# An FFT mixer with two MLPs: conversion slots, stores and first rows at the end of the columns

## The chip, the cores and the metric

The kernel runs on one core of one Trainium2 chip. The metric is the device time of one execution in microseconds (us). Its engines are TensorE (PE, matrix products, with weight loads shown as PEld), VectorE (DVE), ScalarE (ACT), GpSimd (POOL) and SyncE (SP), which here only issues transfers. Each engine and each issuing queue works through its instructions in order.

## The reference

Three blocks follow one another on an input of 4 batches, 3136 positions and 256 channels, all float32.

```python
X = np.fft.rfft(x, axis=1)
x = np.fft.irfft(X * (filt_r + 1j * filt_i)[None], n=3136, axis=1)
h = x.transpose(0, 2, 1) @ U @ V                 # rank 32, along the sequence
u = x + h.transpose(0, 2, 1)
x = u + np.maximum(u @ w_ch1, 0) @ w_ch2         # 256 -> 1024 -> 256
mu, var = x.mean(-1, keepdims=True), x.var(-1, keepdims=True)
xn = (x - mu) / np.sqrt(var + 1e-6) * g_ln
return x + np.maximum(xn @ w2_ch1, 0) @ w2_ch2   # the second MLP has its own weights
```

## The kernel before

The FFT over 3136 positions is done in factors, as matrix products with tables. Batch 0 goes through class `First` ahead of everything else: `rows` makes the first factor, seven steps; `columns` the other factors, the filter and the way back. The result of batch 0 lies in DRAM, `bd[0]`; from there it is read in units of 448 positions (tile `wt`, with a table `ic`). `unit` makes the last factor of the way back, adds `h`, and splits the sum into a high and a low float32r part (`ah`, `al`). The two layers of the MLP (`m1` L792, `m2` L811 to L820) use three products for each, high by high, high by low and low by high. The other three batches run their FFT between the steps of the MLPs.

The weights V, w1, w2 and those of the second MLP come as 64-bit words and are converted on the chip, 18 jobs, in the generator `stagger`: each `next(pr)` is a slot. The first four slots only ask for the words of the first jobs. After them every fourth slot (PACE) starts a job, and every slot moves all jobs under way by one step (`to32`): two copies on ScalarE (L947, L948), four word operations on VectorE (L934 to L940, one slot each), a product and a sum on GpSimd (L952, L954), two idle slots, the high part on ScalarE (L224), the low part (L1026 for weights, L1070 for V). The low part is made on VectorE up to the end of the columns, on GpSimd after that. Jobs 0 and 1 are V; their parts are stored in `vd` (L1061), the low one a slot after it is made, and `load_v` (L1079) reads both back into `v_sb`, issued by GpSimd. `fetch` asks for the words of coming jobs (L928); during the columns it does not go past six. How many slots pass at which place is set by hand: FETCHES and FETCH, ROWSLOTS (a slot for each entry, after that step of the rows), COLSLOTS (so many after each step of the columns).

`columns` works on seven pairs, the last pair first, in ten steps. Step j runs `across` of pair 6-j (transposes L677 into two PSUM banks, copied by ScalarE to `z0`), `forward` of pair 7-j (L689 into two of three rotating PSUM banks; then `filtered`: four products on VectorE, L631 and L636, and four combinations on GpSimd, L638 and L639), and `back` of pair 9-j (L650, then `pt` L657; both need the combinations). For odd indices the products go to rotating tiles `hl` and `hh`, three each, which V's low and high parts use as well. After `back` ScalarE copies the two banks to `be`, a part of `big`, and four stores (L668) go to `bd[0]`, by SP; for pair 0 VectorE makes one of the copies and ScalarE issues two of the stores. Steps 0 to 3 also hold the stages of U (`u_half`: transpose, products, `uf` on VectorE, four copies `uq` on ScalarE). Each step also asks for the filters of a later pair (L602, for the last pair L610 too).

At pair 0, ahead of its own stores, `load_unit` (L729) asks for units 0 and 1: their tables, and the rows from QUICK on, which come from the other six pairs. After the columns follow `finish(0)` (the sum of `pt`, split into `tk`), `late_rows` (L735, the first QUICK rows of units 0 and 1, which pair 0's stores write), the words up to job 7, REST constant products on TensorE (L1172), and then units 0 and 1 and the main loop, with two slots in each step.

## Time and profile before

| what | value |
|---|---|
| median of 3 runs | 1335.75 us (1335.61 to 1335.92) |
| the profiled execution | 1335.85 us |
| its span, first to last instruction | 1334.0 us |
| mean granted TensorE clock | 0.996 of 2.4 GHz |
| TensorE busy | 98% of the span |
| VectorE, ScalarE, GpSimd busy | 60%, 32%, 11% |

All times of the rows are counted from the first instruction. A row of a time line has start, duration, engine, line, operation, what is written from what, and how many instructions were merged into it; in square brackets stands how long the engine sat idle before it and what ended that.

### The profile page before, as it was taken

Reading aid. Unit: us, or ns where it says so; the run is one execution under the profiler, and the core shown is the slowest. Engines: PE = TensorE matmul, PEld = TensorE weight load, DVE = VectorE, ACT = ScalarE, POOL = GpSimd, SP = SyncE. Lnnn points to the kernel's source line nnn. Section 1 sums busy time; section 2 is a strip of 40 time slices with the busy share of each in tenths; the row PEclk is TensorE's granted clock in tenths of the full one; section 3 lists DMA queues with packets and bytes.
Section 4 is the critical chain, followed back from the end, with each engine's and each line's share of the span. In section 5 each row is a group of like instructions: output and inputs, shape, how many; then the busy total and the mean of one; then the engine's idle time right before and its main releaser. Section 6 shows DMA issues by size and latency. Waiting matters only on the chain.

```text
span 1334.0 us, 23246 instructions
## 1 busy us (share of the span) xinstructions
PE 1308.9 (98%) x9018; PEld 1039.6 (78%) x9018; DVE 798.0 (60%) x1620; ACT 424.3 (32%) x831; POOL 149.3 (11%) x128
## 2 busy tenths in 40 slices
PE   8899999999999999999999999999999999999998
PEld 8477677776877877777777877878888888888887
DVE  6937885666656556566565565565455545555454
ACT  4535642333322323323232232232222222222222
POOL 1716540112000011010000010100000000000000
PEclk9899999999999999999999999999999999999999
DMA  9753446576554254453555454522102212210121
GB/s 253 201 160 118 125 126 196 167 209 190 137 179 149 72 145 141 124 145 90 153 171 142 133 168 105 152 78 65 39 27 65 65 18 65 65 44 5 48 48 40
DMA packets 166999, 154.24 MB, mean 116 GB/s; under 512 B 65801, under 2 KB 142473, under 8 KB 166889
## 3 DMA queue, kind: packets, MB, share of 16 engines
q1 hardware_dynamic: 166348, 151.12, 40.8%
q0 software_dynamic: 288, 1.40, 0.5%
q8 instruction: 71, 1.16, 0.4%
q14 instruction: 40, 0.32, 0.1%
q10 hardware_dynamic: 252, 0.23, 0.1%
HBM read 92.71 MB, written 48.97 MB: 106 GB/s over the span
## 4 chain that ended last, share of the span: by engine, by line
PE 87%; DVE 6%; DMA 2%; ACT 2%; issue 1%; POOL 1%; SPq 1%; DVEq 0%; POOLq 0%; ACTq 0%
PE psh L792 38%; PE pso L819 13%; PE pso L820 7%; PE pso L811 6%; PE pso L812 6%; PE pso L813 6%; PE psu L769 2%; PE ps L316 2%; PE ps L390 1%; PE ps L356 1%; PE psu L774 1%; DVE hl L796 1%; PE pt L396 1%; PE ps L650 1%; PE pz L531 1%
## 5 line engine op out<-in xcount | busy, mean ns | idle before, releaser
L796 DVE SCALAR_TENSOR_TENSOR hl<-psh,hh 128x512 fp32r<-128x512 f32 (+1 forms) x400 | 271.7, 680 | 366.2 <-ACT hh L795 365.3
L795 ACT ACTIVATE hh<-psh 128x512 fp32r<-128x512 f32 (+1 forms) x400 | 235.3, 589 | 666.6 <-PE psh L792 666.5
L819 PE MATMUL pso<-wb,hh 128*128 128x512 f32 x784 | 285.0, 397 | 0.7 <-DVE x L834 0.3
L792 PE MATMUL psh<-ah,wb 128*128 128x512 f32 (+1 forms) x800 | 280.1, 391 | 1.9 <-DVE hl L796 1.9
L820 PE MATMUL pso<-wb,hl 128*128 128x256 f32 x784 | 219.8, 280 | 0.0
L792 PEld LDWEIGHTS psh<-ah,wb 128*128 128x128 f32 x800 | 149.8, 188 | 47.6 <-issue 5.3
L819 PEld LDWEIGHTS pso<-wb,hh 128*128 128x128 f32 x784 | 147.3, 188 | 36.2 <-DVE x L834 1.6
L792 PE MATMUL psh<-ah,w1h 128*128 128x512 f32 (+1 forms) x400 | 157.7, 394 | 2.1 <-ACT ah L224 2.1
L811 PE MATMUL pso<-hh,w2h 128*128 128x512 f32 (+1 forms) x400 | 156.7, 392 | 1.0 <-ACT hh L795 0.7
L812 PE MATMUL pso<-hl,w2h 128*128 128x512 f32 (+1 forms) x400 | 154.3, 386 | 2.0 <-DVE hl L796 2.0
L792 PE MATMUL psh<-al,w1h 128*128 128x512 f32 (+1 forms) x400 | 156.0, 390 | 0.2
L792 PE MATMUL psh<-al,wb 128*128 128x512 f32 (+1 forms) x400 | 155.6, 389 | 0.0
L813 PE MATMUL pso<-hh,w2l 128*128 128x512 f32 (+1 forms) x400 | 154.3, 386 | 1.1 <-POOL w2l L1026 1.1
L792 PE MATMUL psh<-ah,w1l 128*128 128x512 f32 (+1 forms) x400 | 154.9, 387 | 0.0
L820 PEld LDWEIGHTS pso<-wb,hl 128*128 128x128 f32 x784 | 148.0, 189 | 7.7 <-DVE hl L796 0.3
L372 POOL TENSOR_TENSOR xs<-xs,ft 128x512 f32<-128x512 f32 x42 | 56.9, 1355 | 643.6 <-DMA xs<-zc 356.4
L792 PEld LDWEIGHTS psh<-ah,w1h 128*128 128x128 f32 x400 | 75.5, 189 | 24.6 <-issue 4.0
L859 DVE SCALAR_TENSOR_TENSOR x2t<-pso,ln,x2t 128x256 f32<-128x256 f32 x196 | 89.7, 479 | 3.7 <-PE pso L820 0.2
L811 PEld LDWEIGHTS pso<-hh,w2h 128*128 128x128 f32 x400 | 75.1, 188 | 21.5 <-issue 5.9
L812 PEld LDWEIGHTS pso<-hl,w2h 128*128 128x128 f32 x400 | 75.2, 188 | 17.6 <-DVE hl L796 2.7
L813 PEld LDWEIGHTS pso<-hh,w2l 128*128 128x128 f32 x400 | 75.2, 188 | 16.7 <-POOL w2l L1026 1.7
L792 PEld LDWEIGHTS psh<-ah,w1l 128*128 128x128 f32 x400 | 75.6, 189 | 15.9
(144 smaller groups left out, 1318.9 us busy)
## 6 DMA issues: line engine op xcount, KB each, us to landing
ft<-flt SPq DMA_DIRECT2D x42, 512.0 KB
xd<-x SPq DMA_DIRECT2D x96, 128.0 KB
x2t<-xd SPq DMA_DIRECT2D x24, 512.0 KB
wt<-bd SPq DMA_DIRECT2D x52, 224.0 KB
out<-x2t SPq DMA_DIRECT2D x84, 128.0 KB
xs<-zc SPq DMA_DIRECT2D x168, 64.0 KB
xt<-x SPq DMA_DIRECT2D x84, 112.0 KB
zd<-ze SPq DMA_DIRECT2D x84, 112.0 KB
```

Of the source, the lines that this page charges most:

```text
L316: nc.tensor.matmul(pss[j][quarter(h), m * D:(m + 1) * D], ct[rows56(j), 2 * h + m], xs[h][rows56(j), m], start=True, stop=True)
L372: nc.gpsimd.tensor_tensor(out=xs, in0=xs, in1=fi[:, e], op=ALU.mult)
L769: nc.tensor.matmul(pss[h][c * HALF:(c + 1) * HALF, dh, h * spare + m:h * spare + half:UW], t[rows, m, d0:d0 + HALF], ic[rows, m, :], start ...
L792: nc.tensor.matmul(ps[:, :n], w[:, kt, fs], a[:, kt, :n], start=j == 0, stop=j == 3 * KT - 1)
L795: nc.scalar.activation(out=hh[:, :n], in_=ps[:, :n], func=AF.Relu)
L796: nc.vector.scalar_tensor_tensor(out=hl[:, :n], in0=ps[:, :n], scalar=0.0, in1=f32(hh[:, :n]), op0=ALU.max, op1=ALU.subtract)
L811: nc.tensor.matmul(o, wh[:, f, ds], hh[:, :n], start=f == 0, stop=False)
L812: nc.tensor.matmul(o, wh[:, f, ds], hl[:, :n], start=False, stop=False)
L813: nc.tensor.matmul(o, wl[:, f, ds], hh[:, :n], start=False, stop=f == FT - 1)
L819: nc.tensor.matmul(o, hh[:, cs], w, start=f == 0, stop=False, skip_group_check=True)
L820: nc.tensor.matmul(o[:, D:], hl[:, cs], w[:, :D], start=False, stop=f == FT - 1, skip_group_check=True)
L859: nc.vector.scalar_tensor_tensor(out=o, in0=acc[c][:, half * D:(half + 1) * D], scalar=rs[:, c:c + 1], in1=o, op0=ALU.mult, op1=ALU.add)
```

## The change

In the rows, three of nine slots are taken out. In the columns the slots are 2 in steps 0 to 5 and 1 in steps 6 to 9 (16), where they were 2, 3, 3, 3, 3, 1 (15). Six slots (WAIT) are run behind the columns, after `finish(0)` and the first rows, and ahead of the constant products, of which 24 are left of 48. So 28 slots have passed when the main loop begins, where it was 24. The limit of six on words fetched in the columns is gone, and with it the fetch up to job 7 after them. A pair's four groups of rows leave in two stores, one for each half, out of one piece of `big` that holds both groups; the bytes are the same. The tables of units 0 and 1 are asked for at pair 1, behind its stores; their rows from QUICK on at pair 0, behind its stores; the first rows where they were.

```diff
-ROWSLOTS = (1, 2, 2, 3, 4, 5, 5, 5, 6)
-COLSLOTS = (2, 3, 3, 3, 3, 1)
+ROWSLOTS = (1, 2, 2, 3, 4, 5)
+COLSLOTS = (2, 2, 2, 2, 2, 2, 1, 1, 1, 1)
-REST = 48
+REST, WAIT = 24, 6
@@ back(p)
-                to = bd[0].rearrange("(j a s g p) w -> a g j p s w", j=2, a=n // 2, s=2, g=2)[p]
+                to = bd[0].rearrange("(j a g p) w -> a j p g w", j=2, a=n // 2, g=4)[p]
+                be = self.big[:, p % 2, 4 * D * ((p + 1) // 2):4 * D * ((p + 3) // 2)]
+                for g in range(2):
+                    (nc.vector.tensor_copy if p == 0 and g else acopy)(
+                        be.rearrange("p (s g k q) -> p s g k q", s=2, g=2, k=KT)[:, :, g], pss[g].rearrange("p (s q k) -> p s k q", s=2, k=KT))
+                for h in range(2):
+                    (nc.scalar if p == 0 and h else nc.sync).dma_start(to[h], be[rows56(h)].rearrange("p (g w) -> p g w", g=4))
+                if p == 1:
+                    for u in range(2):
+                        wt[u] = new_unit(u)
                 if p == 0:
-                    load_unit(0)
-                    load_unit(1)
-                for g in range(2):
-                    at = BLK * (p + 1)
-                    be = self.big[:, g, at:at + BLK]
-                    (nc.vector.tensor_copy if p == 0 and g else acopy)(be.rearrange("p (s k q) -> p s k q", s=2, k=KT),
-                                                                       pss[g].rearrange("p (s q k) -> p s k q", s=2, k=KT))
-                    for h in range(2):
-                        (nc.scalar if p == 0 and h else nc.sync).dma_start(to[g, h], be[rows56(h)].rearrange("p (s w) -> p s w", s=2))
+                    for u in range(2):
+                        first_rows(u, QUICK, QT)
@@
-    def late_rows():
+    def first_rows(u, a, z):
         rows = bd[0].rearrange("(h q m) w -> h q m w", h=2, m=NM)
+        for h in range(2):
+            nc.sync.dma_start(wt[u][0][h * HALF + a:h * HALF + z], rows[h, a:z, UW * u:UW * u + UW])
@@ stagger
-                fetch(min(i + 2, 6) if held.get("columns") else i + 2 if i > 1 else i + 1)
+                fetch(i + 2 if i > 1 else i + 1)
@@ after the columns
-        late_rows()
-        held.pop("fetch")(8)
+        for u in range(2):
+            first_rows(u, 0, QUICK)
+        for _ in range(WAIT):
+            next(pr)
         warm = inner("warm")
         for _ in range(REST):
             nc.tensor.matmul(warm[:, :P], ones, ones, start=True, stop=True)
```

## Rows read from the trace of the kernel before

**Rows 1.** The page: busy time, share of the span and instructions of each engine.
```profile
PE 1308.9 (98%) x9018; PEld 1039.6 (78%) x9018; DVE 798.0 (60%) x1620; ACT 424.3 (32%) x831; POOL 149.3 (11%) x128
```

**Rows 2.** Time line of TensorE, from the constant products on.
```profile
76.64 10.98 PE L1172 MATMUL warm<-ones 128*128 128x128 f32 x96
87.56 1.15 PE L769 MATMUL psu<-ic,wt 56*64 56x56 f32 x64
88.64 0.74 PE L774 MATMUL psu<-v_sb,tk 96*128 96x256 f32 x4
...
90.44 1.14 PE L769 MATMUL psu<-ic,wt 56*64 56x56 f32 x60 [0.80 <-DVE al L227]
...
93.22 0.50 PE L792 MATMUL psh<-ah,w1h 128*128 128x512 f32 x1 [0.98 <-ACT ah L224]
...
101.01 0.50 PE L813 MATMUL pso<-hh,w2l 128*128 128x512 f32 x1 [1.07 <-POOL w2l L1026]
```

**Rows 3.** Time line of the SP queue, at the end of the columns.
```profile
73.68 1.67 SPq L668 DMA_DIRECT2D bd<-big  x4
...
77.06 0.80 SPq L729 DMA_DIRECT2D wt<-bd  x2
...
80.49 1.83 SPq L668 DMA_DIRECT2D bd<-big  x2
84.61 1.29 SPq L735 DMA_DIRECT2D wt<-bd  x4
```

**Rows 4.** Stretches: busy time (instructions) of each engine, clock, DMA share, GB/s.
```profile
30.00:40.00 10.00, 6.11 (x87) 4.02 (x88) 8.47 (x11) 6.10 (x13) 6.19 (x7) 0.95 0.98 263
```

**Rows 5.** Time line of TensorE, in the columns.
```profile
30.42 1.14 PE L677 MATMUL psz<-ident,big 128*120 128x128 f32 x8 [1.26 <-ACT z L224]
...
39.52 1.96 PE L677 MATMUL psz<-ident,big 128*120 128x128 f32 x8 [3.20 <-ACT z L224]
...
67.34 1.07 PE L689 MATMUL ps<-z,s_sb 56*32 56x256 f32 x24 [0.95 <-DVE hh L636]
```

**Rows 6.** Time line of ScalarE, in the columns.
```profile
29.19 0.68 ACT L948 ACTIVATE cyl<-stg 128x512 f32<-128x512 uint32 x1
...
50.68 1.59 ACT L224 ACTIVATE uq<-uf 64x224 f32<-64x224 f32 x4 [2.71 <-DVE uf L572]
```

**Rows 7.** Time line of VectorE, in the columns and behind them.
```profile
47.45 0.69 DVE L631 TENSOR_TENSOR hl<-ps,f 128x512 f32<-128x512 f32 x1 [1.36 <-PE pt L657]
...
60.88 0.68 DVE L631 TENSOR_TENSOR hl<-ps,f 128x512 f32<-128x512 f32 x1
...
80.56 0.42 DVE L227 TENSOR_TENSOR tk<-tt,tk 32x256 fp32r<-32x256 f32 x1 [0.50 <-ACT tk L224]
...
97.60 0.42 DVE L940 TENSOR_SCALAR cyh<-ct 128x512 int32<-128x512 int32 x1
...
101.27 1.67 DVE L938 SCALAR_TENSOR_TENSOR ct<-cyh,ct 128x512 int32<-128x512 int32 x1
```

**Rows 8.** Time line of GpSimd, in the columns.
```profile
58.09 1.18 POOL L639 TENSOR_TENSOR ya<-ya,xs 128x256 f32<-128x256 f32 x1
...
62.03 1.30 POOL L1079 DMA_DIRECT2D v_sb<-vd  x2
...
65.39 1.18 POOL L639 TENSOR_TENSOR ya<-ya,xs 128x256 f32<-128x256 f32 x1
67.34 0.73 POOL L638 TENSOR_TENSOR hl<-hl,hh 128x256 f32<-128x256 f32 x1 [0.76 <-DVE hh L636]
...
70.09 0.74 POOL L638 TENSOR_TENSOR hl<-hl,hh 128x256 f32<-128x256 f32 x1
```

**Rows 9.** The last filter loads (SP time line); the landing of V's load (tile `vd`).
```profile
57.91 1.81 SPq L610 DMA_DIRECT2D f<-flt  x4
...
DMA to landing us min/median/max: 7.0/7.3/7.6
```

**Rows 10.** Stretches: TensorE busy (instructions), granted clock, DMA share, GB/s.
```profile
40.00:42.00 2.00, 2.00 (x15) 0.50 1.01 295
```

More of the change, by code (lines that the diff above doesn't have):

```diff
@@ L727, in load_unit @@
         for h in range(2):
-            q = QUICK if i < 2 else 0
-            nc.sync.dma_start(wt[i][0][h * HALF + q:h * HALF + QT], rows[h, q:, m0:m0 + UW])
-    def late_rows():
+            nc.sync.dma_start(wt[i][0][rows56(h)], rows[h, :, m0:m0 + UW])
+    def first_rows(u, a, z):
         rows = bd[0].rearrange("(h q m) w -> h q m w", h=2, m=NM)
-        for i in range(2):
-            for h in range(2):
-                nc.sync.dma_start(wt[i][0][h * HALF:h * HALF + QUICK], rows[h, :QUICK, UW * i:UW * i + UW])
+        for h in range(2):
+            nc.sync.dma_start(wt[u][0][h * HALF + a:h * HALF + z], rows[h, a:z, UW * u:UW * u + UW])
     def unit(i):
@@ L975, in fetch @@
                 fetched += 1
-        held["fetch"] = fetch
         for n in range(4):
```

## The prediction

> **What bounds the kernel now.** I read the page's busy table first: TensorE works 98% of the span [rows 1], so what is left lies where TensorE waits, and the diff touches only the first hundred microseconds. The time line of TensorE there [rows 2] shows the largest piece: after the last pair of columns it runs 48 constant products from 76.64 to 87.6, and unit 0 begins at 87.56 without a wait of its own. The SP queue tells what the products cover [rows 3]. The last pair leaves TensorE just before 76.64. Its first half's store stands behind two loads of tables and four of rows; those rows wait for the store of the pair before (issued up to 75.35, landed by 77.06, so 1.7 us), and the last store goes out only from 80.49 to 82.32. The rows that need it are asked for at 84.61, 2.3 us later. Then the time line inside the columns: TensorE waits 1.26 us at 30.42 and 3.20 us at 39.52 for ScalarE's copies, and 0.95 us at 67.34 for VectorE [rows 5], which has each pair's products behind two or three conversion slots. After unit 1, which waits 0.80 us for unit 0's split, the first layer begins at 93.22 and waits once for a converted weight, 1.07 us at 101.01 [rows 2].
>
> I sum in times of this profiled execution: 1335.85 us, of which 1334.0 are the span; it lies 0.10 us over the median of the runs shown. A shift of the first layer's start moves the end by as much, since TensorE has no slack behind it.
>
> **Slots in the rows and columns.** A job takes a new slot in four; its ScalarE copies are in its slot 0, VectorE's four word operations in 1 to 4, GpSimd's product and sum in 4 and 5, the high and low parts in 8 and 9. Six slots instead of nine pass before the columns. I count nothing for the rows themselves, where TensorE fills its waits with constant products. But slot 8 (a high part of V and two word copies) no longer stands ahead of the first column copy on ScalarE, which it holds up until 29.87 [rows 6], and the wait at 30.42 [rows 5] shrinks by about 1.15 us. In step 1 the same three copies come back between U's copies and the next column copy, so the 3.20 us wait stays, only 1.15 us sooner.
> Step 3 takes that away again. Slot 12 now falls there: V's second high part and two word copies queue on ScalarE behind U's four copies (50.68, 1.59 us [rows 6]), and VectorE's low part waits for them. Adding these up, I get pair 3's products at 54.4, about where they were. From step 4 on there are two slots where there were three, then one. Pair 2's products come at 59.1 instead of 60.88 [rows 7]. They could be at 58.7, but the three rotating tiles `hl` now hold V's parts at other places, and the first product must wait for TensorE's `pt` of two pairs earlier, as at 47.45, where that costs 1.36 us [rows 7]. Pair 1's follow near 64 and pair 0's near 67. If nothing else held them, the columns would end 2.3 us sooner, near 74.4.
>
> **A wait that is new: `load_v` on GpSimd.** It is still issued after step 4. Before, V's low part had long been stored by then, and the two issues took 1.30 us without a wait [rows 8]. Now that part is made in slot 13 and stored in slot 14, in the same step, and on SP it stands behind a pair's stores and the last eight filter loads, 3.6 us of issues of which the second half is 57.91 to 59.72 [rows 9]. By my times it goes out at 59.9. V's own load took 7.0 to 7.6 us to landing, for far more bytes [rows 9]; the bd stores above 1.7 to 2.3. I take 2.3, the nearest in size, hence 62.2. GpSimd is through with pair 3 at 59.1 (before: 58.09 + 1.18) and waits 3.1 us. Behind the wait stand pair 2's four combinations, a conversion's product and sum, and pair 1's four, and TensorE's back products wait for the combinations. Their prices [rows 8]: 1.30 for the issues, 3.2 for pair 2 (63.33 to 66.57), 2.8 for product and sum (59.27 to 62.03, which used to lie ahead of the load), 2.8 for pair 1 (67.34 to 70.09), in all 72.3; it was 70.09. The back products of pair 1 then start at 70.9 and have their second half's input at 72.3. So the columns end near 76.8: **0.1 us later**, with 74.4 the end without the wait.
>
> **The stores and the first rows.** Merging four stores into two keeps the bytes; both copies must be done before either store, which costs part of a copy, and two issues are saved. On SP the order is now: pair 1's two stores, two tables (0.42 an issue, as the stores of [rows 3]), a load of 512 KB of words that the lifted limit of six lets through (it waits for slot 20's copies on ScalarE, until about 76.4), the last pair's store at 77.0 to 77.4 instead of 80.49, and the four loads of rows that began at 77.06, now to 79.1. The store lands between 79.1 (1.7 us) and, behind the words, 80.0; I take 80.0. First rows: two issues for unit 0 in 0.7 us (four took 1.29 [rows 3]), and landing 1.7 us later at the earliest, 82.4. The other bound is the queue: tables, words, stores and rows are some 2.06 MB from 75.6 on. At the 263 GB/s that a full stretch moved [rows 4] that is 7.8 us, 83.4, and 83.9 with the rest of a landing; at three quarters of that rate 86. I take 83.7, near the full stretch. The 24 products left take 5.5 us (half of 10.98 [rows 2]), end at 82.3 and no longer cover it: TensorE idles 1.4 us. Unit 0 starts at **83.7 instead of 87.56: 3.9 us won.**
>
> **Six slots ahead of unit 0.** They give VectorE six word operations, ScalarE three copies and GpSimd three operations, all behind `finish`, whose last VectorE operation ended at 80.98 [rows 7]. A word operation takes 0.42 alone and up to 1.67 beside GpSimd [rows 7]: 2.5 to 10 us for six, of which at most the last three have GpSimd beside them; I take 4.8, so VectorE is free at 86.0. It wants unit 0's split about when unit 0's products (1.15 + 0.74 [rows 2]) and ScalarE's copy are done, 85.9. Unit 1 needs that split, so **0.3 us lost** (0 to 2.5). The four slots more bring job 4's low weight to completion here, and the wait at 101.01 goes: **1.07 us won.** Later conversions run two steps ahead of where they were; their words are loaded in time either way, and I price that at nothing. Uncovered it would be another wait like that one.
>
> **Sum:** 1335.85 - 3.9 + 0.3 - 1.07 = **1331.2 us**. The columns' 0.1 lies in the 83.7. With the bounds of the landing (82.4 to 86) and of VectorE the likeliest case runs from 1329.6 to 1333.9.
>
> **Rivals.**
> No wait at `load_v` (the store lands while GpSimd is still busy): the columns and SP's order move 2.3 us ahead, **1328.9**. For it: SP could reach the store sooner than I add up. Against: it is behind eight filter loads in a strict order. 22%.
> The clock falls in the gap: with 24 products fewer TensorE has nothing for 1.4 us, and units 0 and 1 are small products with waits. After 3.20 us of idling the granted clock was 0.50, 1.2 GHz [rows 10], and a group of 1.14 us took 1.96 [rows 5]. If it falls by 83, the two units' 1.15 + 0.74 us each [rows 2] grow by 0.72 of themselves, 2.7 us: **1333.9**. Against: the 1.26 us of idling at 30.42 cost nothing that shows. 20%. The Trainium skill (TensorE: Matmul & The Clock Gate, Part 1: The HAM clock gate) states that the throttled state is the default and that activity releases it. By that rule the removed products are a risk and not only a saving, and the result is this rival's; the trace agrees that the clock falls after idling [rows 10].
> `load_v` waits longer: each microsecond past 59.4 goes to the columns' end through GpSimd. Once the store lands after 63.4, TensorE idles over 3 us ahead of pair 1's back products, as at 39.52, and the last 5.9 us of the columns run at 1.2 GHz, 0.72 of that or about 4 us more. At 63.4 this gives 1331.2 + 1.2 + 4 = 1336.4, and at a landing like the longest of V's, 7.6 us [rows 9], 1340.5; between them, **slower: 1338.4**. For it: the queue is full there. Against: 196 KB is a small store. 10%.
>
> **How the numbers follow.** The likeliest case has 48%. The measurement can tell about 0.2% (2.7 us) from no change: faster is below 1333.1. That takes nearly all of the likeliest case and of the first rival and a little of the second, 0.72; slower is the last rival, 0.10; the rest is 0.18. The range 1328.0 to 1334.9 leaves out the slower rival and the edges of the others.
>
> **What would show it.** After: one wait of GpSimd for a `vd` store of about 3 us ahead of `v_sb`, the columns' last `pt` near 76.8, the last store issued near 77, first rows issued near 80, unit 0 at 83 to 84 after a short idle time, the first layer near 89.5, no wait for `w2l`. It is wrong if the columns end near 74.4 (no wait on GpSimd), if the units' products run at 1.2 GHz, if unit 0 starts past 86, or if the units' splits wait for VectorE by more than 1 us.

## The result and the profile after

The changed kernel takes 1344.34 us (median of 4 runs, 1342.6 to 1348.88), the kernel before 1335.68 beside it: 1.007 of the time, 95% interval 1.0045 to 1.0096. By the medians it is **slower by 0.65%**, where 1331.2 was forecast.

The profiled execution after is the longest of the four, 1348.88 us, 4.5 above their median, and its stretches have that in them. I cut the profiled executions at four places on TensorE's time line: the first transpose of the columns (28.09 before, 31.46 after), the first constant product, unit 0, and the first product of the first layer.

| stretch, us | before | forecast | after |
|---|---|---|---|
| columns | 48.55 | 48.7 | 51.69 |
| columns' end to unit 0 (gap) | 10.92 | 6.9 | 9.03 |
| units 0 and 1 | 5.66 | 6.0 | 8.30 |
| first layer to the end | 1240.8 | 1239.7 | 1246.6 |
| span | 1334.0 | 1329.4 | 1347.1 |

The 3.4 us by which the columns begin later are this execution's: two runs that differ only behind the columns (e2 and e9 below) begin them at 28.59 and 28.86, all but one of the others at 27.6 to 30.5. The page, busy times, the line that answers to [rows 1]:

```profile
PE 1313.4 (97%) x8970; PEld 1039.6 (77%) x8970; DVE 797.5 (59%) x1620; ACT 424.8 (32%) x831; POOL 148.8 (11%) x128
```

Time line of TensorE after, answering to [rows 2, 5]:

```profile
32.77 1.14 PE L679 MATMUL psz<-ident,big 128*120 128x128 f32 x8 [0.25 <-ACT z L224]
41.88 1.96 PE L679 MATMUL psz<-ident,big 128*120 128x128 f32 x8 [3.20 <-ACT z L224]
...
75.76 0.66 PE L650 MATMUL ps<-hl,d 64*64 64x256 f32 x8 [2.47 <-POOL hl L638]
...
83.15 5.62 PE L1173 MATMUL warm<-ones 128*128 128x128 f32 x48
92.18 2.39 PE L769 MATMUL psu<-ic,wt 56*64 56x56 f32 x64 [3.40 <-DMA wt<-bd]
94.50 1.22 PE L774 MATMUL psu<-v_sb,tk 96*128 96x256 f32 x4
96.58 1.96 PE L769 MATMUL psu<-ic,wt 56*64 56x56 f32 x60 [0.47 <-DVE al L227]
98.47 1.22 PE L774 MATMUL psu<-v_sb,tk 96*128 96x256 f32 x4
100.47 0.79 PE L792 MATMUL psh<-ah,w1h 128*128 128x512 f32 x1 [0.78 <-ACT ah L224]
```

The two waits at the top of the columns are as forecast. New are 2.47 us ahead of pair 1's way back, 3.40 ahead of unit 0, and durations: a unit's products take 1.96 to 2.39 and 1.22 where they took 1.15 and 0.74. GpSimd's and SP's time lines, answering to [rows 3, 8, 9]:

```profile
67.72 1.30 POOL L1078 DMA_DIRECT2D v_sb<-vd  x2 [6.33 <-issue]
```
```profile
60.81 1.81 SPq L610 DMA_DIRECT2D f<-flt  x4
63.15 0.38 SPq L1060 DMA_DIRECT2D vd<-vl  x1
...
82.77 0.40 SPq L928 DMA_DIRECT2D stg<-w  x1
83.46 0.34 SPq L664 DMA_DIRECT2D bd<-big  x1
83.89 6.71 SPq L735 DMA_DIRECT2D wt<-bd  x8
```

GpSimd is free at 67.72 - 6.33 = 61.39 and waits for V's low part, stored at 63.15; it can go on 4.6 us after that issue. The last store goes out 0.3 us after the columns' end, as forecast, but the eight loads of rows behind it last until 90.6, since the last four wait for it. Stretches after, answering to [rows 4, 10]: the clock stands at 0.50, 1.2 GHz, in pair 1's way back and again from unit 0 into the first layer. A row here has the stretch, its length, the busy time and number of instructions of TensorE, its weight loads, VectorE, ScalarE and GpSimd, then the clock.

```profile
78.00:80.00 2.00, 2.00 (x20) 0.50 (x16) 0.00 (x0) 0.84 (x2) 2.00 (x3) 0.50 0.23 82
...
82.00:92.00 10.00, 6.78 (x70) 5.79 (x60) 7.57 (x13) 4.42 (x9) 2.75 (x3) 0.97 0.85 244
...
100.00:105.00 5.00, 4.53 (x10) 3.43 (x11) 2.00 (x5) 2.29 (x6) 0.00 (x0) 0.50 0.00 0
```

In the kernel before, too, the clock stands at 0.50 for a while, in the first layer behind units whose waits were 0.80 and 0.98 us:

```profile
94.00:97.00 3.00, 3.00 (x8) 2.32 (x9) 0.56 (x2) 0.93 (x3) 0.00 (x0) 0.50 0.00 0
```

The next unit's split is waited for longer than before, first before and then after, and behind that wait the clock of the changed kernel falls once more:

```profile
107.79 0.50 PE L792 MATMUL psh<-ah,w1h 128*128 128x512 f32 x1 [1.10 <-ACT ah L224]
```
```profile
114.97 0.54 PE L792 MATMUL psh<-ah,w1h 128*128 128x512 f32 x1 [2.09 <-ACT ah L224]
```
```profile
115.50:118.50 3.00, 2.98 (x8) 2.39 (x8) 1.09 (x2) 0.81 (x2) 0.00 (x0) 0.50 0.35 104
```

Last, TensorE's waits in the main loop between 160 and 192 us: three in the kernel before,

```profile
163.22 0.50 PE L812 MATMUL pso<-hl,w2h 128*128 128x512 f32 x1 [1.77 <-DVE hl L796]
178.52 1.09 PE L316 MATMUL ps<-xt,ct 56*64 56x256 f32 x14 [0.56 <-DVE hl L796]
179.93 0.50 PE L792 MATMUL psh<-ah,wb 128*128 128x512 f32 x1 [0.33 <-DVE hl L796]
```

and five in the changed kernel, 5.3 us in place of 2.7:

```profile
164.92 0.50 PE L812 MATMUL pso<-hl,w2h 128*128 128x512 f32 x1 [0.26 <-DVE hl L796]
169.34 1.98 PE L1034 MATMUL psw<-wg,ones 128*128 128x512 f32 x4 [1.62 <-DVE hl L796]
173.67 0.50 PE L792 MATMUL psh<-ah,w1h 128*128 128x512 f32 x1 [0.96 <-DVE hl L796]
184.81 0.50 PE L812 MATMUL pso<-hl,w2h 128*128 128x512 f32 x1 [1.10 <-DVE hl L796]
191.37 0.50 PE L792 MATMUL psh<-ah,wb 128*128 128x512 f32 x1 [1.38 <-DVE hl L796]
```

### The profile page after: what moved, and what is told of

It reads as the page before. It is cut to its first block, busy times and chain, and to the rows that moved or that the text cites. A ratio compares the mean times of both kernels' runs of the same rounds, so it can differ in the third digit from the quotient of the medians.

```text
span 1347.1 us, 23130 instructions
## 1 busy us (share of the span) xinstructions
PE 1313.4 (97%) x8970; PEld 1039.6 (77%) x8970; DVE 797.5 (59%) x1620; ACT 424.8 (32%) x831; POOL 148.8 (11%) x128
## 4 chain that ended last, share of the span: by engine, by line
PE 87%; DVE 4%; DMA 3%; ACT 2%; POOL 2%; issue 1%; SPq 1%; DVEq 0%; POOLq 0%; ACTq 0%
PE psh L792 37%; PE pso L819 13%; PE pso L820 6%; PE pso L811 6%; PE pso L812 6%; PE pso L813 6%; PE psu L769 2%; PE ps L316 2%; PE ps L390 1%; PE psu L774 1%; PE ps L356 1%; PE ps L650 1%; PE pz L531 1%; PE pt L396 1%; DVE hl L796 1%
## 5 line engine op out<-in xcount | busy, mean ns | idle before, releaser
L796 DVE SCALAR_TENSOR_TENSOR hl<-psh,hh 128x512 fp32r<-128x512 f32 (+1 forms) x400 | 271.6, 680 | 369.4 <-ACT hh L795 368.3
L792 PE MATMUL psh<-ah,wb 128*128 128x512 f32 (+1 forms) x800 | 280.0, 391 | 2.0 <-DVE hl L796 2.0
L792 PEld LDWEIGHTS psh<-ah,wb 128*128 128x128 f32 x800 | 149.7, 188 | 47.6 <-issue 5.3
L792 PE MATMUL psh<-ah,w1h 128*128 128x512 f32 (+1 forms) x400 | 158.5, 396 | 3.8 <-ACT ah L224 2.9
L792 PE MATMUL psh<-al,w1h 128*128 128x512 f32 (+1 forms) x400 | 156.5, 391 | 0.0
L792 PE MATMUL psh<-al,wb 128*128 128x512 f32 (+1 forms) x400 | 155.5, 389 | 0.0
L792 PE MATMUL psh<-ah,w1l 128*128 128x512 f32 (+1 forms) x400 | 155.4, 388 | 0.0
L792 PEld LDWEIGHTS psh<-ah,w1h 128*128 128x128 f32 x400 | 75.8, 189 | 26.9 <-issue 4.5
L792 PEld LDWEIGHTS psh<-ah,w1l 128*128 128x128 f32 x400 | 75.9, 190 | 16.1
```

What stands on the lines that cost most here:

```text
L792: nc.tensor.matmul(ps[:, :n], w[:, kt, fs], a[:, kt, :n], start=j == 0, stop=j == 3 * KT - 1)
L796: nc.vector.scalar_tensor_tensor(out=hl[:, :n], in0=ps[:, :n], scalar=0.0, in1=f32(hh[:, :n]), op0=ALU.max, op1=ALU.subtract)
```

## The experiments

All runs in one table, read from the time lines. "Slots" are those passed before the main loop, "V" is the issue of V's load counted from the columns' first transpose, "idle" is TensorE's before unit 0, "241st" is the time from the first product of L792 to its 241st, that is, over the first 240. The ratio is to the kernel before, run beside it.

| run | slots | V | columns | gap | idle | units | 241st | ratio (95%) |
|---|---|---|---|---|---|---|---|---|
| before | 24 | 33.9 | 48.55 | 10.92 | 0 | 5.66 | 135.5 | |
| after | 28 | 36.3 | 51.69 | 9.03 | 3.40 | 8.30 | 140.8 | 1.0070 (1.0045 to 1.0096) |
| e1 | 28 | 39.9 | 45.15 | 12.46 | 6.84 | 8.18 | 137.7 | 1.0044 (1.0025 to 1.0063) |
| e2 | 28 | 36.3 | 51.28 | 10.92 | 0 | 5.66 | 140.3 | 1.0050 (1.0033 to 1.0068) |
| e3 | 24 | 32.6 | 47.26 | 10.92 | 0 | 5.67 | 134.2 | 0.9993 (0.9983 to 1.0003) |
| e4 | 28 | 34.8 | 50.08 | 11.69 | 0.70 | 7.05 | 137.9 | 1.0048 (1.0032 to 1.0065) |
| e5 | 28 | 32.6 | 47.17 | 10.91 | 0 | 9.25 | 139.6 | 1.0069 (1.0049 to 1.0090) |
| e6 | 24 | 33.6 | 48.20 | 8.48 | 0.17 | 6.05 | 135.2 | 1.0000 (0.9988 to 1.0011) |
| e7 | 24 | 33.6 | 48.17 | 7.88 | 2.25 | 7.02 | 136.9 | 1.0006 (0.9994 to 1.0018) |
| e8 | 28 | 31.3 | 48.40 | 12.29 | 6.66 | 8.27 | 137.9 | 1.0055 (1.0035 to 1.0074) |
| e9 | 24 | 34.8 | 49.32 | 10.59 | 4.97 | 8.12 | 136.0 | 1.0048 (1.0033 to 1.0063) |
| e10 | 28 | 31.7 | 48.81 | 11.19 | 5.56 | 8.51 | 137.2 | 1.0064 (1.0047 to 1.0081) |
| e11 | 24 | 31.0 | 48.04 | 11.79 | 3.49 | 7.87 | 135.2 | 1.0050 (1.0032 to 1.0069) |
| e12 | 24 | 31.2 | 48.35 | 14.61 | 3.62 | 8.25 | 135.9 | 1.0039 (1.0025 to 1.0052) |
| e13 | 28 | 34.7 | 50.01 | 8.70 | 3.08 | 8.09 | 138.8 | 1.0060 (1.0040 to 1.0080) |
| e14 | 24 | 35.6 | 50.19 | 9.58 | 1.28 | 6.78 | 135.9 | 1.0023 (1.0011 to 1.0035) |
| e15 | 24 | 41.2 | 47.88 | 13.42 | 2.43 | 7.00 | 135.3 | 1.0041 (1.0027 to 1.0056) |
| e16 | 24 | 25.2 | 46.75 | 10.91 | 0 | 5.67 | 134.2 | 0.9992 (0.9980 to 1.0005) |
| e17 | 24 | 26.1 | 47.67 | 8.23 | 0 | 5.89 | 135.1 | 0.9995 (0.9982 to 1.0009) |
| e18 | 24 | 37.3 | 46.89 | 12.83 | 1.85 | 7.02 | 136.9 | 1.0011 (0.9995 to 1.0027) |

The stretches are each of one profiled execution; that of after, e7 and e12 lay 4 to 5.1 us above its run's median, that of e10 and e11 2 to 3.3 below. Up to the columns' end before and e5 are the same code, and their columns differ by 1.4 us; after, e2 and e9 are the same code there, and differ by 2.4. So a difference of 2 us between two rows of that column shows nothing by itself.

### The two halves of the change: e3 and e4

The new stores, tables and rows with the slots of before (diff to the changed kernel):

```diff
-ROWSLOTS = (1, 2, 2, 3, 4, 5)
-COLSLOTS = (2, 2, 2, 2, 2, 2, 1, 1, 1, 1)
+ROWSLOTS = (1, 2, 2, 3, 4, 5, 5, 5, 6)
+COLSLOTS = (2, 3, 3, 3, 3, 1)
-REST, WAIT = 24, 6
+REST = 48
+        held["fetch"] = fetch
-                fetch(i + 2 if i > 1 else i + 1)
+                fetch(min(i + 2, 6) if held.get("columns") else i + 2 if i > 1 else i + 1)
-        for _ in range(WAIT):
-            next(pr)
+        held.pop("fetch")(8)
```


> The kernel before with the stores and loads of the change alone (two stores for a pair, tables at pair 1, rows behind pair 0's stores), slots as before, 48 products kept. All three theories: no time lost, since TensorE still runs 48 products (10.98 us) behind the columns and unit 0 cannot start sooner: 1335 to 1336, and the profile shows when the first rows are asked for, about 80 instead of 84.6. If this part costs by itself, it would be over 1338.

And the slots with the old stores (diff to before):

```diff
-ROWSLOTS = (1, 2, 2, 3, 4, 5, 5, 5, 6)
-COLSLOTS = (2, 3, 3, 3, 3, 1)
+ROWSLOTS = (1, 2, 2, 3, 4, 5)
+COLSLOTS = (2, 2, 2, 2, 2, 2, 1, 1, 1, 1)
-REST = 48
+REST, WAIT = 48, 6
-        held["fetch"] = fetch
-                fetch(min(i + 2, 6) if held.get("columns") else i + 2 if i > 1 else i + 1)
+                fetch(i + 2 if i > 1 else i + 1)
-        held.pop("fetch")(8)
+        for _ in range(WAIT):
+            next(pr)
```


> The kernel before with the slots of the change alone (six in the rows, 2 2 2 2 2 2 1 1 1 1 in the columns, six behind, no limit of six on words), stores and loads as before, 48 products kept. Theory A (load_v): the wait on the stored low part of V is there, GpSimd idles 4 to 6 us before v_sb, the columns end 3 to 5 us later: 1339 to 1343. Theory B (products): no loss, 1334 to 1336. Theory C (slots in the main loop): 1338 to 1340 with the columns ending where they did.

e3 took 1334.79 us, not to be told from before; e4 1342.33, as theory A has it, though its columns are only 1.5 us longer and not 3 to 5. So a loss of 0.48% lies in the slots alone and needs neither the new stores nor the missing constant products; whether these add to it the intervals (0.32 to 0.65% here, 0.45 to 0.96% for the whole change) don't tell.

### Constant products and the clock: e2, e6, e7

The changed kernel with `REST` 48 (e2), and e3 with `REST` 36 (e6) and 24 (e7).

> The changed kernel with 48 constant products again, all else as changed. Theory A (load_v): TensorE's wait inside the columns stays, only the idle time before unit 0 is filled, so at most the units run at full clock: 1341 to 1344. Theory B (products): unit 0 starts about where it did, 92, but at full clock; units and first layer win 3 to 4 us: 1339 to 1341. Theory C (slots): no change, 1344.

> The stores and loads of the change with the slots of before and 36 constant products (8.2 us). With 48 the first rows were asked for by 81.8, columns out at 76.0. If they land within 2.5 us, unit 0 starts at 84.3, right behind the products, 2.7 us sooner than with 48, at full clock: 1332 to 1333. If the rows land later, or the clock falls, 1334 or more.

> The same with 24 products (5.5 us), so ending near 81.5, ahead of the rows. Theory B (the products taken out cost the clock): TensorE idles 2 to 3 us, units 0 and 1 run at 1.2 GHz, some 8 us from unit 0 to the first layer instead of 5.7, and the time is 1 to 3 us above the kernel with 36: 1334 to 1336. If an idle stretch that short leaves the clock alone: as with 36, or 0.5 less, 1331.5 to 1333.

e2 took 1343.07 (theory A's range), e6 1335.81 (1332 to 1333 expected if the clock held; in the units it did), e7 1336.21 us (its theory B, the clock's, had 1334 to 1336). In e2 the units are back at 5.66 us, 2.6 less than after, with the clock at full speed but for the last 0.3 us: that part was the slow clock. But the gap is 1.9 longer, and the main loop stays as long as after. In e7 TensorE idles 2.25 us and the units lose 1.4 of the 3.0 that the gap gains. In e6 gap and units are 2.05 us shorter than before; the ratio is 1.0000. In its profiled execution 1.4 us of that are lost from the first layer to the end (1242.2) and 0.4 by a later begin; no run tells whether the edit or chance does that.

### The six slots and the main loop: e5 and e9

The kernel before with four slots behind the columns (e5), the changed one with four fewer (e9):

```diff
-REST = 48
+REST, WAIT = 48, 4
         held.pop("fetch")(8)
+        for _ in range(WAIT):
+            next(pr)
```


> The kernel before with four more slots run behind the columns, ahead of the constant products, so that the main loop begins with 28 slots passed, as in the changed kernel; nothing else moved. Theory C (the conversions, two steps earlier in the main loop, meet other work there): from the first layer's first product to the end takes 1243 to 1245 us instead of 1240.8, with waits of TensorE at the centering products (psw) near 160 to 170, and the time is 1338 to 1340. Against it: the conversions have room wherever they lie, 1335 to 1336, or the 1.07 us wait for w2l goes and it is 1334.5.

```diff
-REST, WAIT = 24, 6
+REST, WAIT = 24, 2
```


> The changed kernel with WAIT 2 in place of 6: two slots of job 6 wait behind the columns, so 24 and not 28 conversion slots are spent before the main loop; spreading, stores, tables, REST 24 and the order of pair 1's constants stay as changed. Theory A (the two steps' shift of the later conversions is what costs the main loop 2 to 3 us): VectorE's waits in front of TensorE between 160 and 192 us come back from about 5.3 us in all (four waits) to about 2.7 us as in the kernel before, the part from the first main matmul of L792 to the end is 1241 to 1243 us, and the kernel takes 1340 to 1342 us, still slower than before by 4 to 6 us because the columns' wait for the last v_sb (about 6 us) and the slow clock in the units stay. Rival B (the shift is innocent, the tail is long because the clock was low at its beginning): the tail stays at 1245 to 1247 us and the time within 1 us of the changed kernel's, 1343 to 1345 us.

e5 took 1344.91 us, more than its theory gave (1338 to 1340). Part of it, 3.6 us in the units, is its own: unit 1's split stands behind two ScalarE copies that wait for words asked for at 85.83. ScalarE's and TensorE's time lines of e5:

```profile
89.92 0.66 ACT L947 ACTIVATE cyh<-stg 128x512 f32<-128x512 f32 x1 [8.28 <-DMA stg<-w]
```
```profile
92.81 1.96 PE L769 MATMUL psu<-ic,wt 56*64 56x56 f32 x60 [3.29 <-DVE al L227]
...
165.69 1.98 PE L1035 MATMUL psw<-wg,ones 128*128 128x512 f32 x4 [1.64 <-DVE hl L796]
170.03 0.50 PE L792 MATMUL psh<-ah,w1h 128*128 128x512 f32 x1 [0.97 <-DVE hl L796]
181.17 0.50 PE L812 MATMUL pso<-hl,w2h 128*128 128x512 f32 x1 [1.10 <-DVE hl L796]
187.73 0.50 PE L792 MATMUL psh<-ah,wb 128*128 128x512 f32 x1 [1.34 <-DVE hl L796]
```

The last four are the waits of the changed kernel, here with the rows, columns and stores of before. In e9 they go, and the three of before are back; the time, 1343.06 us, stays 1.1 above theory A's range and falls into rival B's, whose 1245 to 1247 us from the first layer to the end are not there (1243.2):

```profile
166.85 0.50 PE L812 MATMUL pso<-hl,w2h 128*128 128x512 f32 x1 [1.78 <-DVE hl L796]
182.16 1.09 PE L316 MATMUL ps<-xt,ct 56*64 56x256 f32 x14 [0.62 <-DVE hl L796]
183.57 0.50 PE L792 MATMUL psh<-ah,wb 128*128 128x512 f32 x1 [0.32 <-DVE hl L796]
```

Every run with 28 slots shows the four waits; none with 24 does, they have the three of before or only the first of them (e6, e16, e17). Over the first 240 products of L792 the eight kernels with 28 slots take 137.2 to 140.8 us, the twelve with 24 take 134.2 to 136.9: on average 3.2 us more, with the wait for `w2l` already saved in it and with what the clock loses (2.6 more if only the five of each kind are compared whose TensorE idled over 2 us before unit 0). The second fall of the clock, near 115, is not the slots' alone: it is in four of the eight (after, e2, e5, e13) and in two of the twelve (e7, e18). That e9's time lies under that of the changed kernel is likely (1.0048 against 1.0070), but the intervals overlap; the place is shown, its worth in the total only about.

### The wait for V's parts: e1, e8, e10, e11

The changed kernel with `VSTEP = 6` (e1); with `ROWSLOTS` of before and `WAIT` 3, which makes V's parts sooner (e8); with V's low part stored by ScalarE's queue (e10); and that with `WAIT` 2 and `REST` 36 (e11):

```diff
-            nc.sync.dma_start(vo[h][:, :, j * 196:(j + 1) * 196], f32(t).rearrange("p (h n) -> p h n", h=2))
+            (nc.scalar if h and j else nc.sync).dma_start(vo[h][:, :, j * 196:(j + 1) * 196], f32(t).rearrange("p (h n) -> p h n", h=2))
```


> The changed kernel with one edit: V is read back after step 6 of the columns and not after step 4 (VSTEP). Theory A, the wait of GpSimd at load_v (6.3 us idle before v_sb in the changed kernel) is the cause: GpSimd then issues the load after pair 1's combinations, with the store long landed, the 6.3 us wait is under 1 us, TensorE's 2.5 us wait before pair 1's back products goes, the columns end 5 us sooner, and the time falls from 1344.3 to about 1336. Theory B, the 24 products taken out are the cause (TensorE idle 3.4 us before unit 0, units and first layer at 1.2 GHz): the columns gain, but unit 0 still waits at a low clock, and the time stays above 1341. Theory C, the moved conversion slots cost it in the main loop (waits between 110 and 200 us): above 1341 too, with those waits unchanged.

> The changed kernel with the nine slots in the rows of before and three behind the columns, so that 28 slots again pass ahead of the main loop, but V's low part is stored in step 2 and load_v stays after step 4. Theory A (load_v): GpSimd has no wait before v_sb, and V's load does not run beside the last stores either (as it did with load_v after step 6); the columns take 45 to 46 us instead of 51.7, and the time falls to 1335 to 1338, what is left over being the low clock in the units and the main loop's 3 us. If the wait was not the cause, it stays above 1341.

> The changed kernel with one edit: the store of the low part of V's later job is issued by ScalarE's queue instead of SyncE's, where it stood behind the filters' loads. V's load stays where the change has it (VSTEP 4). Theory A (the wait of GpSimd's load of v_sb, 6.3 us in the changed kernel, is the store being late on SyncE, and hits the end of the columns in full): the wait falls under 2 us, the columns (first psz to first warming matmul) take 45 to 48 us in place of 51.7, and the kernel gains 3 to 5 us on the changed one: 1339 to 1341.5 us; it stays slower than before by 3.5 to 6 us, of the main loop's four waits and the clock in the units. Rival B (the wait moves to the load itself or to the stores of the bands behind it, which then wait for it as in the run with VSTEP 6): the columns fall as much but the gap before unit 0 grows from 9.0 to 12 us or more, and the time is 1341.5 to 1344 us.

> The changed kernel with three edits together: V's low-part store on ScalarE's queue, WAIT 2 (24 slots before the main loop) and REST 36 in place of 24. Theory A (the three costs add up: wait for v_sb, shift in the main loop, clock in the units): columns 45 to 48 us, gap 8.5 to 9.5, units 5.7 to 7, tail 1241 to 1243, in all 1333 to 1336 us, that is within 0.2% of the kernel before or faster by up to 3 us. Rival B (some cost is shared or one takes the place of the other): the time stays at 1338 us or more.

They took 1341.46, 1343.14, 1345.93 and 1341.95 us. In each GpSimd's wait is gone. The six executions that have it (after, e2, e4, e9, e13, e14) took 49.3 to 51.7 us for the columns, these four 45.2 to 48.8, and of these only e1 lies far off: the wait is real, but what it is worth lies between 0.5 and 6.5 us. The gap is 2.2 to 3.4 us longer than after and TensorE's idle time 3.5 us or more, so that the units stay mostly at the slow clock. Theory A of all four missed the time, in e8 the columns too (45 to 46 expected); what B and C of e1 have in common held, over 1341 us with shorter columns. Rival B of e11 held; that of e10 only in kind, its gap shorter and its time longer than it said. What the queue of SP waited for in e1 (total, times, longest), and TensorE:

```profile
SPq L735 <- DMA bd<-big: 6.4, 3, 3.1
```
```profile
86.80 2.27 PE L769 MATMUL psu<-ic,wt 56*64 56x56 f32 x64 [6.84 <-DMA wt<-bd]
```

The rows wait 6.4 us in all for stores of `bd`, 1.8 in the changed kernel; V's 1.2 MB, issued at 69.05, land at 76.2 and 78.0, while those stores, from 71.86 on, are under way. e10 also bought a new wait, since SP's filter load now waited for ScalarE's store, 4.5 us until that was issued (53.64) and 2.1 until it had landed:

```profile
SPq L602 <- DMA vd<-vl: 6.6, 1, 6.6
```

### Spreading alone: e12

```diff
-COLSLOTS = (2, 3, 3, 3, 3, 1)
+COLSLOTS = (2, 2, 2, 2, 2, 2, 1, 1, 1)
```


> The kernel before with one edit: the 15 conversion slots of the columns stand as (2,2,2,2,2,2,1,1,1) by step, with all else (V's job before the others, stores in one, REST, tables, 24 slots before the main loop) as before. It is the spreading alone without the extra slots. Theory A (spreading by itself is worth what the wait at the second psz, 1.26 us, shows, and at most 3 us where the vector work behind it moves up): columns 45.5 to 48 us in place of 48.5, gap, units and tail unchanged, 1333 to 1335.5 us. Rival B (the even slots push V's words behind the others and GpSimd's load of v_sb then waits): columns 49 to 52 us, 1336 to 1339 us.

1341.32 us. Neither theory: the columns stay (48.35), and the loss comes behind them. SP's waits and TensorE's time line:

```profile
SPq L668 <- DMA bd<-big: 6.4, 3, 4.4
SPq L735 <- DMA bd<-big: 3.6, 1, 3.6
```
```profile
90.95 2.35 PE L769 MATMUL psu<-ic,wt 56*64 56x56 f32 x64 [3.62 <-DMA wt<-bd]
```

SP's stores now wait 6.4 us for earlier stores to land (1.1 before), one of them 4.4 us, and the first rows come too late even for 48 products; the units follow at the slow clock. So the even spread alone costs 0.25 to 0.52%, and in its trace the loss begins in the queue: no engine holds unit 0.

### Job 7's words: e13 and e14

The changed kernel with the words asked for up to job 6 in the columns (e13), and that with `WAIT` 2 and `REST` 36 (e14):

```diff
+        held["fetch"] = fetch
-                fetch(i + 2 if i > 1 else i + 1)
+                fetch(min(i + 2, 7) if held.get("columns") else i + 2 if i > 1 else i + 1)
+        held.pop("fetch")(8)
         for _ in range(WAIT):
```


> The changed kernel with one edit: during the columns words are asked for up to job 6 only (a limit of seven), and job 7's 512 KB behind the first rows instead of ahead of the last pair's store, where the changed kernel's SyncE issues them at 82.77 us. All else as changed. In the changed kernel the last store is issued at 83.46 and the first rows that need it at 88.97, 5.5 us later; in the run with the new stores and the old slots, where the words come after the rows, it is 4.1 us. Theory A (the words stand in the way of the store's landing, 512 KB at 263 GB/s are 2 us): store to first rows 3.9 to 4.4 us, the gap between columns and unit 0 7.3 to 8.0 us in place of 9.0, TensorE's idle time before unit 0 about 2 us in place of 3.4, and unit 0 or both units partly at the full clock: 1 to 3 us less in all, 1341 to 1343.5 us. Rival B (the landing is set by the loads of the other rows, issued behind the store): store to first rows stays at 5 us or more, the gap at 8.7 or more, the time within 1 us of the changed kernel's, 1343.5 to 1345 us.

> The changed kernel with three edits: job 7's words behind the first rows, WAIT 2 (24 slots ahead of the main loop), REST 36. V's load and its late store stay as changed. Theory A (what is left is the columns' wait for the last v_sb store, 6 us, of which TensorE sees 2 to 3): columns 49 to 52, gap 8.3 to 9 with no more than 0.7 us idle, units 5.7 to 6.5, first main matmul to end 1241 to 1243, in all 1337 to 1340 us: slower than before by 0.1 to 0.3%. Rival B (first rows are late again because of the slots, whatever the words): gap 10.5 to 12, units 8, in all 1341 to 1344 us.

e13 took 1343.13 us. SP's and TensorE's time lines of it:

```profile
79.94 0.34 SPq L664 DMA_DIRECT2D bd<-big  x1
80.38 5.23 SPq L735 DMA_DIRECT2D wt<-bd  x8
85.65 1.33 SPq L928 DMA_DIRECT2D stg<-w  x2
```
```profile
88.33 2.19 PE L769 MATMUL psu<-ic,wt 56*64 56x56 f32 x64 [3.08 <-DMA wt<-bd]
```

From the store to the first rows that need it it is now 4.0 us where it was 5.5, to the end of the rows' issues 5.7 where it was 7.1: theory A so far. But unit 0 starts 2.7 us after that end where it started 1.6 after: behind the rows two jobs' words now move. The gap (8.70) shrank by 0.3 us only, and TensorE still idles 3.08 us, which is rival B; the time again lies in theory A's range. e14 took 1339.21 us, within theory A's range, though its gap (9.58), its units (6.78) and, in the profiled execution, its main loop (1245.0) are each above what that theory gave them. So the total agrees while the parts don't, which I don't take as proof that they add up; 0.23% over before remains, and its columns still have the wait for V.

### V's load alone: e15, e16, e17, e18

The kernel before with `VSTEP` 6 (e15), 3 (e16) and 5 (e18), and e6 with `VSTEP` 3 (e17).

> The kernel before with VSTEP 6 in place of 4: V's parts are read back two steps later, after pair 1's combinations, with all slots, stores and constant products as before. Theory A (V's load, 1.2 MB, disturbs the columns wherever it stands among the filters' loads and the pairs' stores, and disturbs the first rows if it stands at the end): columns 45 to 46.5 us in place of 48.55, but the first rows land later, so that the 48 products no longer cover them: 1.5 us or more of idle time before unit 0, units at the slow clock, unit 0 at 87 to 90 us in place of 87.56, in all 1335 to 1340 us. Rival B (the columns' length is of the slots alone, V's load costs nothing): columns 48 to 49 us, unit 0 at 87.5, the time within 0.1% of before.

> The kernel before with VSTEP 3 in place of 4: V's parts are read back one step earlier, near 53 us, ahead of the last eight filter loads (issued from 56.1 us) instead of behind them (62.03). Nothing else is changed, so the slots and the 24 ahead of the main loop are those of before. Theory A (V's 1.2 MB take 7 us and hold up what is issued on SyncE while they move; only a load that falls between the last filter loads and pair 1's stores costs nothing): the filters of the last pairs land late, VectorE's products wait for them, SyncE's stores wait for earlier transfers, and unit 0 starts 1 us or more later after the end of the columns than the 10.92 us of before, with the units at the slow clock: 1338 to 1343 us. Rival B (the earlier the better, what costs is only a load near the end): columns 46.5 to 48.5 us, gap 10.92, units 5.7, the time that of before or up to 2 us less, 1333.5 to 1336 us.

> The kernel with the new stores, tables and rows, the slots of before, REST 36, and V's load one step earlier (VSTEP 3). Theory A (as for the run of before with VSTEP 3: the early load delays filters and stores): gap over 10 us in place of the 8.48 that the same kernel has with VSTEP 4, idle time before unit 0 over 1.5 us, units at 7 to 8 us, 1338 us or more. Rival B (the early load is out of the way of the stores): columns 46 to 48, gap 8.5, units 5.7 to 6, 1332 to 1335 us, which would be faster than both kernels.

> The kernel before with VSTEP 5: V's load one step later, near 66 to 70 us, behind pair 2's combinations and ahead of pair 1's stores. With the run of VSTEP 6 (unit 0 2.4 us late) it tells where the late side begins. Theory A (harmless until it meets the last pairs' stores and the rows): the load starts some 37 to 40 us after the first column product, and unit 0 comes 0 to 1.5 us later after the columns than before, columns 46.5 to 48.5 us: 1334.5 to 1338 us. Rival B (any move off its place costs, early or late, as much as VSTEP 6): gap over 12.5 us, 1340 us or more.

They took 1341.81, 1333.95, 1334.67 and 1338.23 us. TensorE in e15, then in e18:

```profile
91.76 1.38 PE L769 MATMUL psu<-ic,wt 56*64 56x56 f32 x64 [2.43 <-DMA wt<-bd]
```
```profile
87.85 1.40 PE L769 MATMUL psu<-ic,wt 56*64 56x56 f32 x64 [1.85 <-DMA wt<-bd]
```

With no slot moved, a load 3.4 us later makes unit 0 come 1.9 us later after the columns' end, 7.3 us later 2.5: theory A of e15, but for its columns, 0.7 us shorter than before and not 2 or more, and for its time, 1.8 us above the range; and a little over theory A of e18. e18's runs reach from 1332.9 to 1339.75, so it sits on the edge. A load one step earlier does no harm (rival B of e16 and e17), and the columns of e16 are 1.8 us shorter than before, 0.4 shorter than those of e5 with the slots and the load of before; neither e16 nor e17 can be told from before in time. So the early side, which I had suspected, does not explain e8, e10, e11 and e12, whose load goes out 31 to 32 us after the first transpose. What holds up SP's stores there stays open; moving the slots moves conversions, V's stores and words together.

## Why the prediction was wrong

The forecast of the profiled execution misses by 17.7 us: 3.4 are the later begin of this execution's columns, 3.0 the columns, 2.1 the gap, 2.3 the units, 6.9 the main loop. The median is missed by 13.1; of the begin and the columns, 2.6 and 2.4 us are not in e9, which has the same code that far.

**Slots in the columns: right.** The wait at the second transpose fell from 1.26 to 0.25, the 3.20 stayed, the store of V's low part went out at 63.15 - 3.37 = 59.8 (59.9 forecast), and GpSimd was through with pair 3 at 58.0 (59.1), all three counted with this execution's columns begun where those of before did.

**`load_v`: mechanism right, landing mis-sized.** I took 2.3 us from the nearest stores; GpSimd could go on only after 4.6, and with GpSimd 1.1 us sooner the wait came to 6.3 instead of 3.1. That the columns lose by it e1, e8, e10 and e11 show, by how much only roughly. I had put the longer landing, with the clock falling ahead of pair 1's way back, into a rival at 10%, on the ground that 196 KB is a small store. Its size did not settle it: in five other runs with this wait (e2, e4, e9, e13, e14) GpSimd could go on 3.4 to 4.5 us after the store, and in the kernel before, where this store went out at 41.80, it took 5.5 us to land. The landing is told by sixteen increments of a semaphore. In the changed kernel and those five fifteen of them came within 2.5 us of the issue, about as I had it, and the last after 2.9 to 4.0; in e10 and e11, where ScalarE issued the store while SP issued nothing, all sixteen came within 2.1. So one part in sixteen of the store was late; what held it up no run shows. Nor did the clock's fall take the 3 us of idling that I asked for: it came after a wait of 2.47 us, and the granted clock was 0.50 from 78 to 80.

**Stores and rows: order right, landing wrong.** I let the last store land 2.6 us behind its issue; the rows that need it went out 5.2 us behind it (83.80 to 88.97). I had counted the first rows' bytes in with the queue's. But they may be asked for only when the store has landed, and that was when what stood around it had moved. From the first table at 81.08, tables, words, stores and rows are 2.13 MB (the forecast had 2.06); at the 263 GB/s of [rows 4] they end near 89, and the last rows were asked for from 89 on. Their own landing comes on top. e13 agrees: of the 1.5 us that the rows gained when words were put behind them, 1.1 was lost again between the rows' issue and unit 0. The Trainium skill (DMA: Bandwidth & Descriptors, Queues, rings and completion order) states that a transfer's semaphore increment lands only after all earlier writes of that DMA engine, across its queues. The trace agrees as far as it goes: one of the sixteen increments of V's store came late, after 4.0 us, with filter loads issued just ahead of it; the order of the writes within one DMA engine no run here shows.

**The clock: the second rival's mechanism, with more idling than it priced.** The units took 8.30 us, 2.6 more than before, where it said 2.7, and TensorE idled 3.40 us ahead of them and not 1.4. e2 shows it by itself, and e7 without the slots: 7.02 us after 2.25 of idling. The rule of the Trainium skill that was weighed (TensorE: Matmul & The Clock Gate, Part 1: The HAM clock gate), by which the removed products are a risk, was borne out.

**Six slots ahead of unit 0: no loss where I had 0.3 us, the gain right.** Unit 1 waited 0.47 us for its predecessor's split at the slow clock, and 0.80 as before in e2 at full clock; the wait for `w2l` is gone.

**"Later conversions run two steps ahead, I price that at nothing": wrong, the dearest step.** It cost 3.2 us net on average over the first 240 products where I had booked a gain of 1.07. In the profiled execution it was 5.4: 2.7 more at the waits between 160 and 192, 1.0 more at the split near 115, 0.6 near 225, less the 1.07; the other 2 are the lower clock, at 0.50 to 105 and again near 117 where before it was from 94 to 97. The words were there, as I argued. What stood in the way is other conversion work. VectorE is the third engine of these rows (busy us), from 160 to 192 us in the kernel before and then in the changed one:

```profile
160.00:192.00 32.00, 29.35 (x149) 21.79 (x148) 30.45 (x48) 15.01 (x26) 17.45 (x13) 1.00 0.52 139
```
```profile
160.00:192.00 32.00, 26.67 (x121) 19.49 (x120) 28.74 (x40) 14.97 (x26) 20.78 (x15) 1.00 0.41 99
```

In the kernel before 30.5 of 32 us were in use; counted from the first layer on, the changed kernel uses 27.0 of the same 32 (167.25 to 199.25). So it is not the sum of VectorE's work that grew but its place. The trace shows what stands ahead of the `hl` (L796) that TensorE waits for at 173.67: a conversion's word operation, with no pause between the two. At 184.81 it is the same (L938, from 182.38).

```profile
171.50 1.52 DVE L934 TENSOR_SCALAR cyh<-cyh 128x512 f32<-128x512 f32 x1
172.94 0.68 DVE L796 SCALAR_TENSOR_TENSOR hl<-psh,hh 128x512 fp32r<-128x512 f32 x1
```

The longest but one, 1.38 us at 191.37, is of another kind. VectorE had been idle and waited for ScalarE's `hh`, and that stood behind a conversion's high part, which waited for GpSimd's sum:

```profile
189.48 0.63 ACT L224 ACTIVATE wb<-ct 128x512 fp32r<-128x512 f32 x1 [5.36 <-POOL ct L954]
```
```profile
190.63 0.69 DVE L796 SCALAR_TENSOR_TENSOR hl<-psh,hh 128x512 fp32r<-128x512 f32 x1 [3.26 <-ACT hh L795]
```

These two rows stand in all eight kernels with 28 slots, with idle times of 5.3 to 5.4 and 3.3 us. That the count of slots decides is shown from both sides (e5, e9); no run moved a single conversion.

I also treated the rivals as excluding one another. Three came at once. A late store of V's part held GpSimd and with it the columns, and late rows gave idle time and the slow clock; that V's late load also made the rows late is not shown, since in e8, e10 and e11 it went out 4.5 to 5.3 us sooner than after, counted from the columns' begin, and the rows came later still after the columns' end.

## What to carry to other kernels

A store that other work waits for can land much later than its size says: one of 196 KB took 2.1 us with nothing issued beside it and 5.5 in the kernel before, among other loads. Price it by a row with the same traffic around it, count the bytes that are under way with it, then add the dependent load's own landing. Moving helper work ahead moves it in all later stretches too, so look at what it will now stand in front of on every engine of its chain, and vary that count by itself. Where several stalls can come together, sum them as one case too.

## What was not expected of the hardware

- V's load (1.2 MB) took 6.4 to 10.7 us to land, by the run; before it was [rows 9].
- The units' time grew with TensorE's idle time before unit 0, because more of them ran at 1.2 GHz: 5.7 to 6.05 us at full clock after 0.17 or less, 6.8 after 1.28, 7.0 after 1.85 to 2.43, 7.9 to 8.5 after 3.08 and more (e4, 7.05 after 0.70, and e5, with a wait of its own, stand apart).
- The clock fell without a long wait: in the kernel before it was 0.50 from 94 to 97 us behind waits of 0.80 and 0.98, in the changed one behind waits of 2.47 and 2.09.
- Runs of one kernel spread widely: 25 of the kernel before, beside e16, reach from 1332.16 to 1339.65 us. A gain of 2 us in one stretch could be seen in the trace and not in the time (e6, e16).
